# Attention decode with a cache: the last output row stored as two one-row stores from two engines, and 16 diagnostic loads taken out

## The chip, the cores and the metric

The kernel runs on one core of a Trainium2 chip. The metric is device time in microseconds (us) of one execution. A profiled execution also has a span, from its first to its last instruction, which is about 2.1 us shorter than its device time. In this kernel TensorE does the matmuls, VectorE and ScalarE make the copies, and SyncE issues most of the transfers (DMAs). SBUF is the memory that these load into, and PSUM the one that matmuls write to.

## The reference

Two decode steps for one token, side by side. A: 32 heads over 32768 cached keys. B: 32 query heads on 8 cached heads, over the last 4096 keys. Each ends with a projection from 4096 to 512 numbers, and the output is the two rows joined.

```python
def _A_ref(x, k_cache, v_cache, wq, wo):            # x [1,1,512], caches [1,32,32768,128]
    q = (x @ wq).reshape(1, 1, 32, 128).transpose(0, 2, 1, 3)
    p = softmax(einsum("bhqd,bhkd->bhqk", q, k_cache) * 128 ** -0.5)
    o = einsum("bhqk,bhkd->bhqd", p, v_cache)
    return o.transpose(0, 2, 1, 3).reshape(1, 1, 4096) @ wo        # wo [4096, 512]
# _B_ref: the same with 8 cached heads, each used by 4 query heads, and the last 4096 keys
return concatenate([a, b], axis=-1)                                # [1, 1, 1024], bf16
```

## The kernel before

It streams the caches through SBUF, one A head at a time. When the last head's cache has been asked for, SyncE asks for the output weights of B (two pieces) and A (five, growing smaller, so that little work follows the last one), and then for 16 tiny loads. Load `i` covers `i + 1` partitions with 32 bytes each. They fill a tile that nothing reads; they were put in as a diagnostic.

```python
WO_CUTS = {"A": (0, 11, 19, 25, 29, 32), "B": (0, 16, 32)}
# [...] after the loop over the A heads
for n in ("B", "A"):
    for part in range(len(self.WO_CUTS[n]) - 1):
        self.load_wo(n, part)
for i in range(16):
    self.load(self.marks[0:i + 1, 16 * i:16 * i + 16], self.X["A"]["wo"][0:i + 1, 0:16], self.marksem[i])
self.emit_spread("A")
self.emit_proj()
for i in range(16):
    self.op("sp", lambda e, i=i: e.wait_ge(self.marksem[i], 16))
for n in ("B", "A"):
    self.op("sp", lambda e, n=n: e.wait_ge(self.outsem[n], 16))
```

The projections: B first, whose four strips are summed by one more matmul; then A. Most of A's row is made as two halves of 256 columns, in partitions 0 and 64 of the PSUM bank `psPT`, by two matmuls that run side by side. One VectorE copy and one store of two rows, both 512 bytes, end the program.

```python
def halves(self, e, bank, lhsT, rhs, begin, end):
    for i in range(2):
        inst = e.matmul(bank[64 * i:64 * i + 1, 0:256], lhsT=lhsT, rhs=rhs[:, 256 * i:256 * i + 256], start=begin,
                        stop=end, tile_position=(0, 64 * i), skip_group_check=True)
    return inst

def store(self, name, bank, off, dep):
    o = self.op("dve", lambda v: v.tensor_copy(self.out_sb[0:65, :], bank[0:65, 0:256]), dep)
    self.op("sp", lambda e: e.dma_start(self.out[0, :, off:off + 512].rearrange("a (i x) -> (a i) x", i=2),
                                        self.out_sb[0:65:64, :]).then_inc(self.outsem[name], 16), o)

def emit_proj(self):
    # [...] B's 32 matmuls into self.S, in four strips
    strips = self.op("dve", lambda v: v.tensor_copy(self.pb[:, :], self.S[:, :]), o)
    rows = o = self.op("pe", lambda e: e.matmul(self.ACC[0:1, :], lhsT=self.e32[:, 0:1], rhs=self.pb[:, :], ...), strips, self.accread)
    # [...] B's copy and its store, one row of 1024 bytes, from SyncE
    row = self.proj_part("A", 0, lambda e, lhsT, rhs, a: e.matmul(self.T[1][0:1, :], ...))
    row = self.op("dve", lambda v: v.tensor_copy(self.pb[0:1, :], self.T[1][0:1, :]), row, rows)
    for part in range(1, len(self.WO_CUTS["A"]) - 1):
        if part == 3:
            self.op("pe", lambda e: self.halves(e, self.PT, self.e32[0:1, 0:1], self.pb[0:1, :], False, False), row)
        o = self.proj_part("A", part, lambda e, lhsT, rhs, a: self.halves(e, self.PT, lhsT, rhs, a == top, a == 31))
    self.store("A", self.PT, 0, o)
```

Of the kernel before, what the change touches and what calls it, by code (L numbers as in the profile page):

```python
# [3 lines left out]
BF16 = mybir.dt.bfloat16  # L4
F32 = mybir.dt.float32
ALU = mybir.AluOpType
ACTF = mybir.ActivationFunctionType
AXX = mybir.AxisListType.X

DH = 128  # L10
NQH = 32
STRIPS = 4
HALF = 128
# [40 lines left out]
class _Kernel:  # L54
# [118 lines left out]
    def emit(self, eng):  # L173
# [22 lines left out]
        def body(e):  # L196
# [30 lines left out]
            for k, plan in enumerate(plans):  # L227
                for p, q in zip(plan, plans[-1]):
                    assert p == q or (k == 0 and set(p) <= set(q)), (eng, k, p, q)
# [37 lines left out]
    def alloc(self):  # L267
        nc = self.nc
        sb = nc.alloc_sbuf_tensor
        self.kbuf = sb("kbuf", [128, 3 * HALF * DH], BF16, align_bytes=4096)  # L270
        self.vbuf = sb("vbuf", [128, 2 * HALF * DH], BF16, align_bytes=4096)
        self.kt = [sb(f"kt{i}", [128, 1024], BF16) for i in range(NKT)]
        self.psb = sb("psb", [128, 512], BF16)
        self.ptsb = sb("ptsb", [128, 512], BF16)
        self.ident = sb("ident", [128, 128], BF16)
        self.ones = sb("ones", [128, 128], BF16)
        self.e32 = sb("e32", [128, 32], F32)
        self.spread = sb("spread", [32, 4 * 129], BF16)
        self.tr = {k: sb(f"tr_{k}", [128, 32], F32) for k in ("in", "a")}
        self.rows64 = sb("rows64", [128, 64], F32)  # L280
        self.nscale = sb("nscale", [1, 128], F32)
        self.m4 = sb("m4", [1, 128], F32)
        self.pb = sb("pb", [128, 512], F32)
        self.out_sb = sb("out_sb", [128, 256], BF16)
        self.marks = sb("marks", [16, 17 * 16], BF16)
        self.c = {}
        for name, d in self.X.items():
            HG = d["HG"]
            self.c[name] = dict(
                x=sb(f"x_{name}", [128, 12], BF16),  # L290
                oc=[sb(f"oc_{name}{i}", [128, DH + 1], F32) for i in range(2 if name == "B" else 1)],
                b=sb(f"b_{name}", [128, 32], F32),
                cm=sb(f"cm_{name}", [128, 32], F32),
                mr=sb(f"mr_{name}", [1, HG], F32),
                nb=sb(f"nb_{name}", [128, 2], F32),
                hot=sb(f"hot_{name}", [128, d["nb"]], F32),
                lh=sb(f"lh_{name}", [128, HG], F32),
                hsel=sb(f"hsel_{name}", [128, 64], F32),
                rinv=sb(f"rinv_{name}", [32, 1], F32),
                ob=sb(f"ob_{name}", [32, DH], BF16),  # L300
                oz=sb(f"oz_{name}", [128, 32], BF16),
            )

        self.qz = sb("qz", [128, 32 * self.X["B"]["NKVH"] + 64], BF16)
        self.qa = sb("qa", [128, NQH], BF16)
        self.qrow = sb("qrow", [128, 512], BF16)
        self.qw = sb("qw", [128, 64], BF16)
        self.hw = sb("hw", [128, 32], F32)
        ps = nc.alloc_psum_tensor
        self.S = ps("psS", [128, 512], F32)  # L310
        self.T = [ps(f"psT{i}", [128, 512], F32) for i in range(NT)]
        self.PT = ps("psPT", [128, 512], F32)
        self.ACC = ps("psACC", [128, 512], F32)
        self.G = ps("psG", [128, 512], F32)
        s = nc.alloc_semaphore
        self.ksem = [s(f"ksem{i}") for i in range(2)]
        self.vsem = [s(f"vsem{i}") for i in range(2)]
        self.xsem = {n: s(f"xsem_{n}") for n in self.X}
        self.wosem = {n: [s(f"wosem_{n}{i}") for i in range(len(self.WO_CUTS[n]) - 1)] for n in self.X}
        self.outsem = {n: s(f"outsem_{n}") for n in self.X}  # L320
        self.marksem = [s(f"marksem{i}") for i in range(16)]



# [69 lines left out]
    def plan(self):  # L394
        self.lsem = {"k": self.ksem, "v": self.vsem}
        self.fill = {w: [0, 0] for w in "kv"}
        self.free = {"k": [None] * 3, "v": [None] * 2}
        self.nbatch = 0
        self.copies = []
        self.pending = []  # L400
        self.psread = self.ptread = self.sread = self.accread = None
        self.gath = self.qcopy = self.hcopy = self.qread = None
        self.constants()
        a, b = self.X["A"], self.X["B"]

        self.load_wq("B")
        self.load_b("k", 0)
        self.load_wq("A")
        self.load_b("k", 1)
        self.emit_qproj("B")  # L410
        self.emit_unit("B", 0)
        self.emit_qproj("A")
        self.emit_stats("B", 0)
        self.emit_unit("B", 1, {1: lambda: self.emit_PT("B", 0)})
        self.emit_stats("B", 1)
        for g in range(2):
            if g == 1:
                self.emit_PT("B", g)
            self.load_b("v", g)
            self.emit_PV("B", g)  # L420
        self.emit_spread("B")

        for g in range(NQH):
            self.loop = {"pe": g, "dve": g // 2}
            self.load_k(g, 1 if 0 < g < NQH - 1 else 2)
            self.load_v(g)
            self.emit_qcopy(g)
            self.emit_unit("A", g)
            self.emit_stats("A", g)
            self.emit_PT("A", g)  # L430
            self.emit_PV("A", g)
        self.loop = {}
        for n in ("B", "A"):
            for part in range(len(self.WO_CUTS[n]) - 1):
                self.load_wo(n, part)
        for i in range(16):
            self.load(self.marks[0:i + 1, 16 * i:16 * i + 16], self.X["A"]["wo"][0:i + 1, 0:16], self.marksem[i])
        self.emit_spread("A")
        self.emit_proj()
        for i in range(16):  # L440
            self.op("sp", lambda e, i=i: e.wait_ge(self.marksem[i], 16))
        for n in ("B", "A"):
            self.op("sp", lambda e, n=n: e.wait_ge(self.outsem[n], 16))

    def constants(self):
# [264 lines left out]
    def proj_part(self, name, part, out):  # L710

        a0, a1 = self.WO_CUTS[name][part:part + 2]
        oz, wo = self.c[name]["oz"], self.kbuf[:, HALF * DH * self.wo_third(name):]
        def mm(e):
            inst = None
            for a in range(a0, a1):
                inst = out(e, oz[:, a:a + 1], wo[:, 512 * a:512 * a + 512], a)
            return inst
        return self.op("pe", mm, (self.wosem[name][part], 16), self.c[name]["ozop"])

    def halves(self, e, bank, lhsT, rhs, begin, end):

        for i in range(2):
            inst = e.matmul(bank[64 * i:64 * i + 1, 0:256], lhsT=lhsT, rhs=rhs[:, 256 * i:256 * i + 256], start=begin,  # L724
                            stop=end, tile_position=(0, 64 * i), skip_group_check=True)
        return inst

    def store(self, name, bank, off, dep):
        o = self.op("dve", lambda v: v.tensor_copy(self.out_sb[0:65, :], bank[0:65, 0:256]), dep)  # L729
        self.op("sp", lambda e: e.dma_start(self.out[0, :, off:off + 512].rearrange("a (i x) -> (a i) x", i=2),  # L730
                                            self.out_sb[0:65:64, :]).then_inc(self.outsem[name], 16), o)

    def emit_proj(self):

        top = self.WO_CUTS["A"][1]
        for part in range(len(self.WO_CUTS["B"]) - 1):
            o = self.proj_part("B", part, lambda e, lhsT, rhs, a: e.matmul(
                self.S[32 * (a % 4):32 * (a % 4) + 1, :], lhsT=lhsT, rhs=rhs, start=(a < 4), stop=(a >= 28),
                tile_position=(0, 32 * (a % 4)), skip_group_check=True))
# [3 lines left out]
        o = self.op("dve", lambda v: v.tensor_copy(self.qrow[0:1, :], self.ACC[0:1, :]), o)  # L743
        self.op("sp", lambda e: e.dma_start(self.out[0, :, 512:1024], self.qrow[0:1, :]).then_inc(self.outsem["B"], 16), o)
        row = self.proj_part("A", 0, lambda e, lhsT, rhs, a: e.matmul(
            self.T[1][0:1, :], lhsT=lhsT, rhs=rhs, start=(a == 0), stop=(a == top - 1), skip_group_check=True))
        row = self.op("dve", lambda v: v.tensor_copy(self.pb[0:1, :], self.T[1][0:1, :]), row, rows)
        for part in range(1, len(self.WO_CUTS["A"]) - 1):
            if part == 3:
                self.op("pe", lambda e: self.halves(e, self.PT, self.e32[0:1, 0:1], self.pb[0:1, :], False, False), row)  # L750
            o = self.proj_part("A", part, lambda e, lhsT, rhs, a: self.halves(e, self.PT, lhsT, rhs, a == top, a == 31))
        self.store("A", self.PT, 0, o)

# [1 line left out]
_INS = ['A_x', 'A_k_cache', 'A_v_cache', 'A_wq', 'A_wo', 'B_x', 'B_k_cache', 'B_v_cache', 'B_wq', 'B_wo']  # L755
# [24 lines left out]
```

## Time and profile before

| | before |
|---|---|
| device time, median of 3 | 1324.14 us (1323.98 to 1324.18) |
| span of the profiled run | 1322.0 us |
| HBM read | 570.43 MB at 432 GB/s |
| last A weights land, from the span's start | 1318.87 us |
| from there to the end | 3.09 us |

Lines of the profile's page of the kernel before: the span, the mean busy share of the 16 DMA engines in 40 equal slices (in tenths), and the traffic.

```profile
span 1322.0 us, 28805 instructions
...
DMA  9999999999999999999999999999999999999998
...
HBM read 570.43 MB, written 0.00 MB: 432 GB/s over the span
```

The transfers are never below 9 tenths before the last slice. The kernel is as long as its loads, plus what follows the last one. The end of the chain of waits of the kernel before (start, duration, what) shows which load that is:

```profile
1286.51 32.36 DMA kbuf<-in_A_wo_dram
1318.87 0.04 issue
1318.92 0.51 PE psPT L724 x6
1319.43 0.02 issue
1319.45 0.42 DVE out_sb L729
```

The same end in the timeline of the kernel before (start, duration, engine, line, operation, and in brackets the idle time ahead of it with what ended it; SPq is SyncE's queue, where a DMA's issue is shown):

```profile
1287.37 20.63 SPq L326 DMA_DIRECT2D marks<-in_A_wo_dram  x15
...
1313.40 0.24 SPq L744 DMA_DIRECT2D out_dram<-qrow  x1
...
1318.92 0.20 PEld L724 LDWEIGHTS psPT<-kbuf,oz_A 128*1 128x1 bf16 x6 [0.58 <-DMA kbuf<-in_A_wo_dram]
1318.92 0.49 PE L724 MATMUL psPT<-kbuf,oz_A 128*1 128x256 bf16 x6 [0.29 <-DMA kbuf<-in_A_wo_dram]
1319.45 0.42 DVE L729 CAST out_sb<-psPT 65x256 bf16<-65x256 f32 x1 [3.71 <-PE psPT L724]
1319.90 0.59 SPq L730 DMA_DIRECT2D out_dram<-out_sb  x1
```

TensorE waits for the weights, then come copy, issue, flight and the program's end. The diagnostic loads (`marks`) are issued while SyncE has nothing else to do. The one-row store of B takes SyncE 0.24 us to issue, the two-row store of A 0.59 us.

### The profile page before, as it was taken

Reading aid. Unit: us, or ns where it says so; the run is one execution under the profiler, and the core shown is the slowest. Engines: PE = TensorE matmul, PEld = TensorE weight load, DVE = VectorE, ACT = ScalarE, POOL = GpSimd, SP = SyncE. Lnnn points to the kernel's source line nnn. Section 1 sums busy time; section 2 is a strip of 40 time slices with the busy share of each in tenths; the row PEclk is TensorE's granted clock in tenths of the full one; section 3 lists DMA queues with packets and bytes.
Section 4 is the critical chain, followed back from the end, with each engine's and each line's share of the span. In section 5 each row is a group of like instructions: output and inputs, shape, how many; then the busy total and the mean of one; then the engine's idle time right before and its main releaser. Section 6 shows DMA issues by size and latency. Waiting matters only on the chain. (4 is left out here: it accounts for less than half of the span.)

```text
span 1322.0 us, 28805 instructions
## 1 busy us (share of the span) xinstructions
PE 966.2 (73%) x13243; PEld 674.9 (51%) x13243; DVE 751.3 (57%) x1341; ACT 54.8 (4%) x167; POOL 2.6 (0%) x22
## 2 busy tenths in 40 slices
PE   4675668777767877677787876778787677868686
PEld 3453446555444655444465544446554444655453
DVE  3663456665545666554566655556655555666463
ACT  0000000000000000000000000000000000000000
POOL 0000000000000000000000000000000000000000
PEclk8887798888779887877988788798878878888798
DMA  9999999999999999999999999999999999999998
GB/s 404 434 435 435 436 432 436 434 436 434 431 436 436 428 438 434 430 438 432 434 436 432 434 434 434 436 432 434 437 430 436 436 430 436 434 432 436 432 434 359
DMA packets 13489, 570.60 MB, mean 432 GB/s; under 512 B 1827, under 2 KB 1830, under 8 KB 2214
## 3 DMA queue, kind: packets, MB, share of 16 engines
q1 hardware_dynamic: 13190, 570.44, 99.8%
q8 instruction: 8, 0.13, 0.0%
q10 hardware_dynamic: 288, 0.00, 0.0%
q14 instruction: 3, 0.02, 0.0%
HBM read 570.43 MB, written 0.00 MB: 432 GB/s over the span
## 5 line engine op out<-in xcount | busy, mean ns | idle before, releaser
L563 DVE COPY kt<-psT 128x1024 bf16<-128x1024 bf16 x1056 | 654.9, 684 | 237.5 <-PE psT L559 235.7
L559 PE MATMUL psT<-ident,kbuf 128*128 128x128 bf16 x8448 | 579.1, 234 | 168.5 <-DMA kbuf<-in_A_k_cache_dram 154.6
L559 PEld LDWEIGHTS psT<-ident,kbuf 128*128 128x128 bf16 x8448 | 539.3, 106 | 261.0 <-DMA kbuf<-in_A_k_cache_dram 162.7
L662 PE MATMUL psACC<-vbuf,ptsb 128*4 128x512 bf16 (+1 forms) x2112 | 185.2, 527 | 23.2 <-ACT ptsb L637 21.3
L582 PE MATMUL psS<-kt,qw 128*32 128x512 bf16 x2048 | 157.6, 384 | 15.3 <-DVE kt L563 15.3
L676 DVE TENSOR_SCALAR oc_A<-psACC,hot_A 128x128 f32<-128x128 f32 x32 | 11.2, 351 | 250.1 <-PE psG L689 250.1
L662 PEld LDWEIGHTS psACC<-vbuf,ptsb 128*4 128x4 bf16 (+1 forms) x2112 | 60.4, 110 | 138.2 <-issue 91.0
L610 ACT ACTIVATE psb<-psS,nb_A 128x512 bf16<-128x512 f32 x32 | 22.0, 687 | 1165.4 <-DVE nb_A L609 1165.4
L582 PEld LDWEIGHTS psS<-kt,qw 128*32 128x32 bf16 x2048 | 34.0, 95 | 57.9 <-DVE kt L563 31.3
L689 PE MATMUL psG<-oc_A,hw 128*32 128x128 f32 (+1 forms) x128 | 19.3, 227 | 52.3 <-DVE oc_A L678 52.3
L689 PEld LDWEIGHTS psG<-oc_A,hw 128*32 128x32 f32 x128 | 11.4, 109 | 62.4 <-DVE oc_A L678 55.1
L634 PE MATMUL psPT<-ident,psb 128*128 128x128 bf16 x136 | 18.0, 275 | 34.0 <-ACT psb L610 34.0
L678 DVE SCALAR_TENSOR_TENSOR oc_A<-psACC,hot_A,oc_A 128x128 f32<-128x128 f32 x96 | 33.7, 351 | 3.4
L599 DVE TENSOR_REDUCE tr_in<-psS 128x1 f32<-128x512 f32 x34 | 23.5, 692 | 17.1 <-PE psS L582 17.1
L634 PEld LDWEIGHTS psPT<-ident,psb 128*128 128x128 bf16 x136 | 10.2, 117 | 37.0 <-ACT psb L610 36.7
L603 PE MATMUL psACC<-rows,tr_in 128*1 128x64 f32 x64 | 8.7, 217 | 25.5 <-DVE tr_in L599 25.5
L637 ACT ACTIVATE ptsb<-psPT 128x512 bf16<-128x512 bf16 x34 | 20.3, 597 | 31.1 <-PE psPT L634 31.1
L603 PEld LDWEIGHTS psACC<-rows,tr_in 128*1 128x1 f32 x64 | 2.7, 80 | 35.1 <-DVE tr_in L599 35.1
L607 PE MATMUL psACC<-mr_A,nscale 1*128 1x1 f32 x64 | 12.1, 256 | 9.7 <-DVE mr_A L606 9.7
L607 PEld LDWEIGHTS psACC<-mr_A,nscale 1*128 1x128 f32 x64 | 9.4, 182 | 15.7 <-DVE mr_A L606 15.7
L609 DVE COPY nb_A<-psACC 128x1 f32<-128x1 f32 x32 | 5.0, 157 | 15.0 <-PE psACC L607 15.0
L501 PE MATMUL psACC<-vbuf,x_B 128*2 128x512 bf16 x32 | 3.6, 627 | 13.5 <-DMA x_B<-in_B_x_dram 13.5
(81 smaller groups left out, 75.7 us busy)
## 6 DMA issues: line engine op xcount, KB each, us to landing
kbuf<-in_A_k_cache_dram SPq DMA_DIRECT2D x4, 4096.0 KB, 22.2
kbuf<-in_B_k_cache_dram SPq DMA_DIRECT2D x2, 4096.0 KB, 31.7
vbuf<-in_B_v_cache_dram SPq DMA_DIRECT2D x2, 4096.0 KB, 24.7
vbuf<-in_B_wq_dram SPq DMA_DIRECT2D x1, 4096.0 KB, 12.5
vbuf<-in_A_wq_dram SPq DMA_DIRECT2D x1, 4096.0 KB, 32.2
kbuf<-in_B_wo_dram SPq DMA_DIRECT2D x2, 2048.0 KB, 33.3
kbuf<-in_A_wo_dram SPq DMA_DIRECT2D x1, 1408.0 KB, 27.7
kbuf<-in_A_wo_dram SPq DMA_DIRECT2D x1, 1024.0 KB, 29.7
```

The lines of the kernel that those rows point to most:

```text
L559: inst = e.transpose(T[:, 128 * k:128 * k + 128], src[:, DH * k:DH * k + DH], self.ident[:, :])
L563: self.copies.append(self.op("dve", lambda v: v.tensor_copy(KT[:, :], T[:, :]), o, to="pe"))
L582: inst = e.matmul(self.S[32 * c:32 * c + 32, :], lhsT=win, rhs=self.kt[(bb + c // 2) % NKT][:, 512 * (c % 2):512 * (c % 2) + 512], start=b ...
L599: o = dve(lambda v: v.reduce_max(tr["in"][:, 0:1], self.S[:, :], axis=AXX), self.sdone, self.k_pool, to="pe" if name == "A" else None)
L603: o = self.op("pe", lambda e: e.matmul(self.ACC[0:1, 0:64], lhsT=tr["in"][:, 0:1], rhs=self.rows64[:, :], start=True, stop=True, skip_grou ...
L607: o = self.op("pe", lambda e: e.matmul(self.ACC[:, 64:65], lhsT=self.nscale[:, :], rhs=t["mr"][0:1, :], start=True, stop=True, skip_group_ ...
L610: self.sread = self.op("act", lambda s: s.activation(out=self.psb[:, :], in_=self.S[:, :], func=ACTF.Exp, bias=t["nb"][:, k:k + 1], scale= ...
L634: inst = e.transpose(PT[:, 128 * jj:128 * jj + 128], self.psb[:, 128 * jj:128 * jj + 128], self.ident[:, :])
L637: self.ptread = self.op("act", lambda s: s.activation(out=self.ptsb[:, :], in_=PT[:, 0:512], func=ACTF.Copy), self.psread, to="pe")
L662: inst = e.matmul(acc[32 * c:32 * c + rows, 0:512], lhsT=lhsT, rhs=rhs, start=begin, stop=end, tile_position=(0, 32 * c), skip_group_check ...
L678: o = self.op("dve", lambda v, src=src, hot=hot: v.scalar_tensor_tensor(out=oc, in0=src, scalar=hot, in1=oc, op0=ALU.mult, op1=ALU.add), p ...
L689: return self.op("pe", lambda e: e.matmul(self.G[0:32, c0 + c:c0 + c2], lhsT=win, rhs=t["oc"][g % len(t["oc"])][:, c:c2], start=False, sto ...
```

## The change

Its intent: drop the diagnostics, and shorten the end. Each half of the row gets its own matmul signal, its own copy (VectorE and ScalarE side by side) and its own one-row store (from SyncE and ScalarE).

```diff
 [...]
-        for i in range(16):
-            self.load(self.marks[0:i + 1, 16 * i:16 * i + 16], self.X["A"]["wo"][0:i + 1, 0:16], self.marksem[i])
         self.emit_spread("A")
         self.emit_proj()
-        for i in range(16):
-            self.op("sp", lambda e, i=i: e.wait_ge(self.marksem[i], 16))
-        for n in ("B", "A"):
+        for n in self.outsem:                    # "B", "A0", "A1"
             self.op("sp", lambda e, n=n: e.wait_ge(self.outsem[n], 16))
 [...]
-    def store(self, name, bank, off, dep):
-        o = self.op("dve", lambda v: v.tensor_copy(self.out_sb[0:65, :], bank[0:65, 0:256]), dep)
-        self.op("sp", lambda e: e.dma_start(self.out[0, :, off:off + 512].rearrange("a (i x) -> (a i) x", i=2),
-                                            self.out_sb[0:65:64, :]).then_inc(self.outsem[name], 16), o)
+    def store(self, bank, i, dep):
+        row = slice(64 * i, 64 * i + 1)
+        out, src = self.out_sb[row, :], bank[row, 0:256]
+        if i == 0:
+            o = self.op("dve", lambda v: v.tensor_copy(out, src), dep)
+        else:
+            o = self.op("act", lambda e: e.activation(out=out, in_=src, func=ACTF.Copy), dep)
+        self.op("act" if i else "sp", lambda e: e.dma_start(self.out[0, :, 256 * i:256 * i + 256], out).then_inc(
+            self.outsem[f"A{i}"], 16), o)
 [...]
-            o = self.proj_part("A", part, lambda e, lhsT, rhs, a: self.halves(e, self.PT, lhsT, rhs, a == top, a == 31))
-        self.store("A", self.PT, 0, o)
+            self.proj_part("A", part, lambda e, lhsT, rhs, a: self.halves(e, self.PT, lhsT, rhs, a == top, False)
+                           if a < 31 else None)
+        oz, wo = self.c["A"]["oz"], self.kbuf[:, HALF * DH * self.wo_third("A"):]
+        for i in range(2):
+            o = self.op("pe", lambda e, i=i: self.halves(e, self.PT, oz[:, 31:32], wo[:, 512 * 31:512 * 32], False, True, (i,)),
+                        (self.wosem["A"][-1], 16), self.c["A"]["ozop"])
+            self.store(self.PT, i, o)
```

More of the change, by code (lines that the diff above doesn't have):

```diff
@@ L284, in alloc @@
         self.out_sb = sb("out_sb", [128, 256], BF16)
-        self.marks = sb("marks", [16, 17 * 16], BF16)
         self.c = {}
@@ L319, in alloc @@
         self.wosem = {n: [s(f"wosem_{n}{i}") for i in range(len(self.WO_CUTS[n]) - 1)] for n in self.X}
-        self.outsem = {n: s(f"outsem_{n}") for n in self.X}
-        self.marksem = [s(f"marksem{i}") for i in range(16)]
+        self.outsem = {n: s(f"outsem_{n}") for n in ("B", "A0", "A1")}
     def load(self, dst, src, sem, *deps):
@@ L716, in mm, with halves @@
             for a in range(a0, a1):
-                inst = out(e, oz[:, a:a + 1], wo[:, 512 * a:512 * a + 512], a)
+                inst = out(e, oz[:, a:a + 1], wo[:, 512 * a:512 * a + 512], a) or inst
             return inst
-        return self.op("pe", mm, (self.wosem[name][part], 16), self.c[name]["ozop"])
-    def halves(self, e, bank, lhsT, rhs, begin, end):
-        for i in range(2):
+        deps = (self.wosem[name][part], 16), self.c[name]["ozop"]
+        return self.op("pe", mm, *deps)
+    def halves(self, e, bank, lhsT, rhs, begin, end, only=(0, 1)):
+        for i in only:
             inst = e.matmul(bank[64 * i:64 * i + 1, 0:256], lhsT=lhsT, rhs=rhs[:, 256 * i:256 * i + 256], start=begin,
```

## The prediction

> **What bounds the kernel now.** Its loads. The page shows 570.43 MB read from HBM at 432 GB/s over 1322.0 us, and the DMA row of the 40 slices stands at 9 tenths in all but the last. The chain of waits agrees for the end: 32.36 us of it is the last piece of the A output weights, landing at 1318.87. Only what follows can shrink: TensorE 0.51 us, VectorE's copy 0.42 (from 1319.45), the store's issue on SyncE 0.59 (from 1319.90), its flight, and the program's end at 1321.96. That is 3.1 us, 0.23%.
>
> **Removed: 16 diagnostic loads.** The timeline shows SyncE issuing them from 1286.99 to 1308.0, behind all the A weights; SyncE has nothing else to do then. Their 136 packets of 32 bytes follow the weights on each DMA engine, so the weights should not land sooner. Their completions run until 1320.64 and hold back the B store (issued 1313.40, complete 1320.53), which isn't last. The A store's packets start at 1321.13, 0.64 us after its issue ends; the very first load, on empty queues, needed 0.61 (0.43 to 1.04). So the loads don't hold up the A store either. The waits for them occupy SyncE from 1320.53 to 1320.99, but the A store completes only at 1321.49: hidden. Removal alone: 0.0 us (up to 0.1).
>
> **Changed at the end.** The two last matmuls ran side by side (starts 1319.135 and 1319.138), so a signal for each half gains nothing. VectorE's copy of 1x256 should cost what 65x256 does (1x512 took 0.68 us, 128x512 0.69): 0.42 us. ScalarE: 0.195 us for one column and 0.687 for 512 give an estimate of 0.44 for 256, so it is ready with VectorE or 0.03 later.
>
> The gain is in the issue: 0.59 us for the two-row store, 0.24 for the one-row B store. A one-row store should start its packet 0.35 us sooner. The Trainium skill ("DMA: Bandwidth & Descriptors", "Why a DMA increments its semaphore by 16 and not by 1") has such a store use one engine, the sequencer adding the other counts; the trace agrees: the B store is one packet of 1024 bytes with one completion. The same page ("Issuing engines are not separate DMA queues") says that issuing from two engines saves only sequencer time. Simultaneous issues from both at the start took 0.34 to 0.59 us, so I allow 0.1 us for the pair's interference. Both packets go to one engine, 0.03 us each. The completion that ends the program is probably ScalarE's.
>
> **Sum.** 0.35 less 0.03 to 0.1: 0.25 to 0.3 us, 0.02%. From 1324.14 I predict 1323.86 us; 8 in 10 between 1323.3 and 1324.3. Faster by over 2%: 0.003; within 2%: 0.994; slower: 0.003.
>
> **What would show it.** Right: the last weights land at 1318.9 again; copies on VectorE and ScalarE overlap, 0.42 to 0.44 us; each store's issue takes 0.25 to 0.4; last completion about 1321.2, span 1321.7; the B store completes near 1315. Wrong: weights over 0.2 us sooner (the loads did cost something), or an issue on ScalarE of 0.6 us.
>
> **What would make it wrong.** A reload of ScalarE's table before its copy (1.28 us at the start; in the loop it copies without one); the two issues taken one after the other; a different pace of the loads over 1320 us, where 0.05% exceeds the whole change.

## The result, and the profile after

The changed kernel took 1323.68 us (median of 6, 1323.58 to 1326.17) and the kernel before 1324.16 us (median of 6, 1323.98 to 1324.72). The ratio is 1.0, 95% interval 0.9987 to 1.0013: the same, by that measure. It isn't the ratio of the medians, which is 0.9996: the means of the six runs are equal (1324.22 us each), since one run at 1326.17 us pulls that of the changed kernel up.

Lines of the page after:

```profile
span 1321.6 us, 28783 instructions
...
DMA  9999999999999999999999999999999999999998
...
HBM read 570.43 MB, written 0.00 MB: 432 GB/s over the span
```

The load pace is untouched. The end in the timeline after:

```profile
1314.71 0.32 SPq L744 DMA_DIRECT2D out_dram<-qrow  x1
...
1318.89 0.20 PEld L719 LDWEIGHTS psPT<-kbuf,oz_A 128*1 128x1 bf16 x6 [0.26 <-DMA kbuf<-in_A_wo_dram]
1319.42 0.41 DVE L727 CAST out_sb<-psPT 1x256 bf16<-1x256 f32 x1 [2.36 <-PE psPT L719]
1319.45 0.38 ACT L729 ACTIVATE out_sb<-psPT 1x256 bf16<-1x256 f32 x1 [18.04 <-PE psPT L719]
1319.86 0.25 SPq L730 DMA_DIRECT2D out_dram<-out_sb  x1
1319.86 0.58 ACTq L730 DMA_DIRECT2D out_dram<-out_sb  x1
```

The weights are still what TensorE waits for last (0.26 us), but in this execution its weight loads (PEld) sat idle for only 0.26 us there, against 0.58 before. The end of the chain of waits after therefore runs back through TensorE's earlier work and not through the load:

```profile
1316.24 3.15 PE psPT L719 x42
1319.39 0.02 issue
1319.42 0.41 DVE out_sb L727
```

That chain hides a wait which the timeline shows. It is a warning that will matter below: in this execution the loads lead TensorE by very little.

The trace also records when a store's packets (the pieces in which it is moved) start and when its completion (the last count on the semaphore that the program waits for) arrives. All times are us from the span's start:

| step | before | after, half from SyncE | after, half from ScalarE |
|---|---|---|---|
| last A weights land | 1318.874 | 1318.848 | 1318.848 |
| last matmul starts | 1319.138 | 1319.109 | 1319.112 |
| copy starts, takes | 1319.452, 0.421 | 1319.417, 0.411 | 1319.451, 0.375 |
| issue starts, takes | 1319.900, 0.592 | 1319.856, 0.249 | 1319.856, 0.583 |
| first packet starts | 1321.125 | 1320.572 | 1320.683 |
| completion | 1321.493 | 1320.927 | 1321.111 |
| end of the trace | 1321.961 | 1321.585 | 1321.585 |

I call U the time from the start of the last matmul to the end of the trace. It leaves out whatever made that matmul early or late. U fell from 2.823 to 2.473 us, by 0.350 us, and the columns before and ScalarE's give its parts as differences. The copy and what leads to the issue: 0.018 less. Issue to packet: 1.225 to 0.827, 0.398 less. Packet to completion: 0.368 to 0.428, 0.060 more. The end: 0.006 more. So the gain lies between the start of the issue and the first packet.

### The profile page after: what moved, and what is told of

Same layout as the page of the kernel before. It is cut to its first block, busy times and chain, and to the rows that moved or that the text cites. A ratio compares the mean times of both kernels' runs of the same rounds, so it can differ in the third digit from the quotient of the medians.

```text
span 1321.6 us, 28783 instructions
## 1 busy us (share of the span) xinstructions
PE 969.7 (73%) x13243; PEld 676.6 (51%) x13243; DVE 751.8 (57%) x1341; ACT 55.2 (4%) x168; POOL 2.6 (0%) x22
```

## The experiments

My theory was that a one-row store starts its packet sooner than a two-row one and that all else is worth nothing. Rivals: the diagnostic loads were the cost; the copies side by side are the gain. Twelve kernels ran, in three groups, each group on one chip with the kernel before beside it. All gave correct results. The device times differ by less than their scatter, so each profile's U decides, and the times are given beside it. That is one profile per kernel, but U repeats well: it was 2.473 to 2.481 us in the seven profiles of the changed and the reordered end (after, e0, e7 to e11), and 2.816 to 2.847 in the three with a two-row store (before, e1, e3).

| run | U, us | last matmul after last landing, us | median, us | fastest, us |
|---|---|---|---|---|
| before, first profile | 2.82 | 0.26 | 1324.16 | 1323.98 |
| changed, first profile | 2.47 | 0.26 | 1323.68 | 1323.58 |
| group 1: before | | | 1324.31 | 1323.84 |
| e0_after | 2.48 | 1.38 | 1323.86 | 1323.54 |
| e1_no_loads | 2.82 | 0.26 | 1324.02 | 1323.83 |
| e2_loads_kept | 2.46 | 0.79 | 1323.89 | 1323.57 |
| e3_two_row | 2.85 | 0.26 | 1324.09 | 1323.98 |
| group 2: before | | | 1324.09 | 1323.90 |
| e4_both_sync | 2.60 | 0.26 | 1324.05 | 1324.01 |
| e5_both_act | 2.86 | 0.59 | 1324.29 | 1324.10 |
| e6_one_copy | 2.61 | 0.26 | 1324.38 | 1323.82 |
| e7_reorder | 2.48 | 0.26 | 1323.85 | 1323.72 |
| group 3: before | | | 1324.29 | 1323.74 |
| e8_after_again | 2.48 | 0.26 | 1323.82 | 1323.55 |
| e9_reorder_again | 2.48 | 0.26 | 1323.65 | 1323.43 |
| e10_late | 2.48 | 2.58 | 1325.96 | 1324.77 |
| e11_late_reorder | 2.48 | 1.86 | 1325.10 | 1324.17 |

Every ratio to the kernel before had an interval that holds 1 (from 0.9995 for e0_after and e2_loads_kept to 1.0011 for e10_late).

### e0_after: the changed kernel again

No edit. 

> The changed kernel again, unedited, on the same chip as the next three. T is the time from the landing of the last piece of the A output weights to the end of the trace; it was 3.09 us before the change (1318.874 to 1321.961) and 2.74 after it (1318.848 to 1321.585). Both theories: T 2.74 within 0.05; device time 0.3 to 0.5 us under the kernel before.

The time behaved (0.45 us under before, by medians), but the profile fell in an execution of 1324.68 us, and T, the measure I had announced, was 3.86 us and not 2.74. Lines of the timeline of e0_after:

```profile
1319.45 0.63 PEld L719 LDWEIGHTS psPT<-kbuf,oz_A 128*1 128x1 bf16 x14 [0.44 <-issue]
1319.45 0.93 PE L719 MATMUL psPT<-kbuf,oz_A 128*1 128x256 bf16 x14
1320.41 0.41 DVE L727 CAST out_sb<-psPT 1x256 bf16<-1x256 f32 x1 [2.23 <-PE psPT L719]
```

The last 14 matmuls run in one go, with no wait for weights ahead of them; these had landed at 1318.73. TensorE's own chain was late. From its last matmul on, all went as before: U 2.48. My expectation of T was wrong, because I had taken the landing of the weights for the only thing that sets the last matmul's start. From here on I use U, and call an execution lucky when the weights, and not TensorE's chain, come last.

### e1_no_loads: only the diagnostic loads are removed

```diff
 # the kernel before [...]
-        for i in range(16):
-            self.load(self.marks[0:i + 1, 16 * i:16 * i + 16], ..., self.marksem[i])
 [...]
-        for i in range(16):
-            self.op("sp", lambda e, i=i: e.wait_ge(self.marksem[i], 16))
```

> The kernel before without its 16 diagnostic loads and their waits, the last store as it was (one VectorE copy, one two-row store from SyncE). My theory (the gain is in the store's issue; the loads were hidden): T stays 3.09 within 0.06, the time equals the kernel before within 0.15 us, and only the B store's completion moves, from 3.1 us after its packet to about 0.5. Rival (the loads and their waits were the cost): T about 2.75, time 0.35 us or more under before, and the last weights may land sooner.

U 2.816 and T 3.08: the loads and their waits cost nothing, and the rival falls. The median, 0.29 us under that of before, was outside my 0.15; the fastest runs, 1323.83 and 1323.84, agree. Five of the nine runs of before took 1324.31 us or more; no profile was kept of those, so that they were late as e0 was is likely and not shown. B's store completed 0.48 us after its packet, where it had taken 3.22 (packet at 1317.305, completion at 1320.528); with the loads back (e2) it took 3.21. So the loads did hold something up: the completion of B's store, which wasn't last. The weights landed at 1318.655, 0.22 us sooner than before, which is the prediction's own sign that the loads had cost something. But in e2, with all the loads, they landed at 1318.671, so the loads don't explain it. Over all 14 profiles the landing lay between 1318.60 and 1319.07, a scatter of 0.47 us that is larger than the gain.

### e2_loads_kept: only the store is changed

```diff
 # the changed kernel [...]
+        for i in range(16):
+            self.load(self.marks[0:i + 1, 16 * i:16 * i + 16], ..., self.marksem[i])
         self.emit_spread("A")
         self.emit_proj()
+        for i in range(16):
+            self.op("sp", lambda e, i=i: e.wait_ge(self.marksem[i], 16))
```

> The changed kernel with the 16 diagnostic loads and their waits put back. My theory: T about 2.75 to 2.9, time 0.2 to 0.4 us under before. The range allows for this: [...]completions of these loads ran until 1.77 us after the last weights' landing, and the new packets start 1.72 us after it, so the loads that were hidden behind the slow store may show a little behind the fast one. Rival (the loads were the cost): T about 3.09, as before.

U 2.461, the whole gain with all the loads in place. T was 3.25, above the range and indeed above before's, since TensorE's chain was late. The end of the timeline of e2_loads_kept has the issues of the changed kernel:

```profile
1320.20 0.24 SPq L736 DMA_DIRECT2D out_dram<-out_sb  x1
1320.20 0.58 ACTq L736 DMA_DIRECT2D out_dram<-out_sb  x1
```

Why the chain was late can be read here, and it isn't as in e0. B's projection started at 1309.31 us, sooner than in the lucky profile after (1310.26), but its 32 matmuls took 3.31 us in place of 1.90: the granted clock was 0.5 from 1308.80 to 1312.22, and 1.0 there in the profiles of before, after and e0. From the start of B's projection to the last matmul e2 needed 10.15 us, and the two other late profiles, e0 and e5, 8.73. The profile was of a late execution, so the loads had 0.5 us more time to finish; whether they show in a lucky one can be read only from the fastest times, 1323.57 against 1323.54 for the changed kernel: no sign of it.

### e3_two_row: split copies, one two-row store

```diff
 # the changed kernel, store(): both copies as they were, then
-        self.op("act" if i else "sp", lambda e: e.dma_start(self.out[0, :, 256 * i:256 * i + 256], out)...)
+        self.op("sp", lambda e: e.dma_start(self.out[0, :, 0:512].rearrange("a (i x) -> (a i) x", i=2),
+                                            self.out_sb[0:65:64, :]).then_inc(self.outsem["A"], 16), self.half, o)
```

> The changed kernel with its two copies on VectorE and ScalarE, but one two-row store from SyncE that waits for both. My theory: the split copy gains nothing and the two-row issue takes 0.59 us again, so T 3.05 to 3.12 and the time is that of before within 0.15 us. Rival (the copies side by side are the gain): T about 2.75, time 0.35 us under before.

U 2.847, T 3.11. The timeline of e3_two_row:

```profile
1319.34 0.41 DVE L727 CAST out_sb<-psPT 1x256 bf16<-1x256 f32 x1 [2.26 <-PE psPT L719]
1319.38 0.38 ACT L729 ACTIVATE out_sb<-psPT 1x256 bf16<-1x256 f32 x1 [17.97 <-PE psPT L719]
1319.83 0.59 SPq L730 DMA_DIRECT2D out_dram<-out_sb  x1
```

The copies overlap as in the changed kernel, and the two-row issue takes 0.59 us again, its packet 1.227 us after the issue's start. All of the gain is gone. The side-by-side copies by themselves gain nothing.

### e4_both_sync: two one-row stores, both from SyncE

```diff
-        self.op("act" if i else "sp", lambda e: e.dma_start(
+        self.op("sp", lambda e: e.dma_start(
```

> The changed kernel, both one-row stores from SyncE, one after the other. U is the time from the start of the last matmul to the end of the trace: 2.82 us before the change, 2.47 after it, 2.46 with the loads kept, 2.85 with one two-row store. My theory (a one-row issue costs SyncE 0.25 us, and what ends the program is the later store's completion): the second issue starts 0.3 us after the first, so its packet starts about 0.15 to 0.2 us later than ScalarE's did (0.83 us after the first issue's start): U 2.6 to 2.7. Rival (only the number of rows in a store matters, not who issues): U 2.47. Second rival (two rows cost the same however they are issued): U 2.82.

U 2.596, at the near end of the range. Both issues in the timeline of e4_both_sync:

```profile
1320.08 0.54 SPq L730 DMA_DIRECT2D out_dram<-out_sb  x2
```

The second issue started 0.293 us after the first, and each packet came 0.72 us after its own issue. So one-row stores alone are worth 0.23 us of the 0.35, and issuing the second from another engine 0.12. The device times, 1324.05 against 1324.09 for before, don't show the 0.23; in this profile the weights landed at 1319.07, 0.2 us later than before and the latest of all profiles, for which I have no cause.

### e5_both_act: both from ScalarE

```diff
 # the changed kernel, store(): both copies as they were, then
+        for j, d in enumerate((self.half, o)):
+            self.op("act", lambda e, j=j: e.dma_start(self.out[0, :, 256 * j:256 * j + 256],
+                    self.out_sb[64 * j:64 * j + 1, :]).then_inc(self.outsem[f"A{j}"], 16), d)
```

> Both one-row stores from ScalarE, after its copy. It tells why ScalarE's issue took 0.58 us where SyncE's took 0.25. If ScalarE is slow at issuing by itself, two issues take 1.2 us, and U is 2.9 to 3.2. If its 0.58 us was the wait for SyncE's simultaneous issue, each takes 0.25 to 0.3, and U is 2.6 to 2.7, as with both from SyncE.

U 2.856: neither alternative as I put it. Both issues in the timeline of e5_both_act:

```profile
1320.08 0.81 ACTq L731 DMA_DIRECT2D out_dram<-out_sb  x2
```

The first issue took 0.509 us with SyncE silent, the second 0.257. Yet the first packet came 0.751 us after its issue's start, nearly as soon as SyncE's. So ScalarE's first issue is long by itself (the simultaneous one adds 0.07 us), and the length matters for what ScalarE issues next and little for that packet. Why the first is long is left open.

### e6_one_copy: one copy, two one-row stores from SyncE

```diff
-            o = self.op("dve", lambda v: v.tensor_copy(out, src), dep)      # and ScalarE's copy
+        o = self.op("dve", lambda v: v.tensor_copy(self.out_sb[0:65, :], bank[0:65, 0:256]), dep)
+        for j in range(2):
+            self.op("sp", lambda e, j=j: e.dma_start(self.out[0, :, 256 * j:256 * j + 256],
+                    self.out_sb[64 * j:64 * j + 1, :]).then_inc(self.outsem[f"A{j}"], 16), o)
```

> One VectorE copy of 65x256 as before the change, and two one-row stores from SyncE. My theory (the split copy gains nothing): U equal to that of the run with both stores from SyncE and split copies, within 0.04 us. Rival (the split copy gains): U 0.1 us or more longer than that.

U 2.611, 0.015 us from e4's. The split copy is worth nothing; it only has ScalarE's row ready on ScalarE.

### e7_reorder and e9_reorder_again: filling TensorE's idle time

```diff
         strips = self.op("dve", lambda v: v.tensor_copy(self.pb[:, :], self.S[:, :]), o)
+        row = self.proj_part("A", 0, lambda e, lhsT, rhs, a: e.matmul(self.T[1][0:1, :], ...))
         rows = o = self.op("pe", lambda e: e.matmul(self.ACC[0:1, :], ...), strips, self.accread)
 [...]
-        row = self.proj_part("A", 0, lambda e, lhsT, rhs, a: e.matmul(self.T[1][0:1, :], ...))
```

> The changed kernel with one more edit: the 11 matmuls of the first piece of the A projection are issued ahead of the row sum of B, so TensorE has work in the 1.3 us in which it waited for VectorE's copy of B's strips. It tests my reading of the late runs: in three of the six profiles the last matmul started 0.04 us after the last weights' landing plus 0.2 us of earlier matmuls; in the unlucky ones (the changed kernel's repeat was 1.0 us later, the one with the loads kept 0.4) TensorE's chain from the last head was late, with the weights landed as always. If so, this gives a late run back up to about 1 us: U stays 2.47, the last matmul starts 0.25 us after the last landing, median 1323.4 to 1323.7, and fewer runs over 1324. If late runs come from the loads, the spread of its times is as that of the changed kernel, and the last matmul is late by as much as before.

> The reordered kernel once more (its first five runs lay within 0.16 us, but its profile fell in a lucky execution, so they showed little). If the order shortens a late chain by about 1 us: all five within 0.3 us, the same fastest run as the changed kernel within 0.1 us, and a lower or equal median. If its narrow spread was luck: a run 0.5 us or more over the fastest, as with the changed kernel.

(Four, not three, of the six profiles before this run started the last matmul 0.26 us after the landing.) The first five runs lay between 1323.72 and 1323.88, the next five between 1323.43 and 1323.93. The first median missed my 1323.4 to 1323.7. The second set missed too: its spread of 0.50 us is over the 0.3 that I had set and just reaches the 0.5 that I had named as the sign of luck, and its fastest run lies 0.12 us from e8's, not within 0.1; only the median was lower, as expected. Side by side in group 3, the reordered kernel's mean is 1323.68 us and that of the changed one (e8) 1323.97. Over all its sets, the changed kernel had 6 of 16 runs over 1324.0 us; the reordered one had none of 10. These sets mix chips and groups (in group 3 alone it is 2 of 5 against none of 5), so that the order removes late runs is likely and not shown. Both its profiles fell in lucky executions and prove nothing of the cause; the next pair tests what the order is worth when the chain is late.

### e8_after_again: the changed kernel on the chip of group 3

No edit. 

> The changed kernel once more, for the same chip as the next. Two profiles of it so far had the last matmul 0.26 and 1.38 us after the last landing of weights. Expected: fastest run 0.3 to 0.4 us under the fastest of before, U 2.47, and at least one of five runs 0.5 us or more over its fastest, if TensorE's chain is late in some runs as I read it.

Fastest 1323.55 us, 0.19 under the fastest of before (a little less than expected), and two of five runs 0.85 us or more over it, as expected.

### e10_late and e11_late_reorder: a late chain, on purpose

```diff
 # the changed kernel (e10), the reordered kernel (e11)
-        for part in range(len(self.WO_CUTS["B"]) - 1):
+        for part in (0, 0, 0, 1):
```

> The changed kernel with the first half of the B projection done three times instead of once (the result is the same, since each pass starts its sums anew): TensorE's chain is made late by about 1.9 us (two more passes of 16 matmuls; 32 took 1.9 us). If the end is the later of the weights' landing and TensorE's chain, with 1.2 us of slack in a lucky run: time 0.5 to 2.0 us over the changed kernel's, with the weights landing as always and U 2.47. If only the weights' landing counts: the same time.

> The same lateness put into the reordered kernel. If the order fills 1.0 us of TensorE's idle time: 0.8 to 1.1 us under the run with the lateness alone in a case where that one is 1 us or more late, and its last matmul that much nearer to the last landing. If the order gains nothing: the same time as that run.

Weights landed as always (1318.73 and 1318.83), U was 2.48 in both, and the times rose to 1325.96 and 1325.10 us: the first 2.1 us over e8, just past the top of my range, the second 0.86 less. B's projection in the timeline of e10_late, with what TensorE does next:

```profile
1310.85 3.62 PE L737 MATMUL psS<-kbuf,oz_B 128*1 128x512 bf16 x64
...
1315.28 1.02 PE L741 MATMUL psACC<-pb,e 128*1 128x512 f32 x2 [0.80 <-DVE pb L740]
...
1316.13 2.11 PE L745 MATMUL psT<-kbuf,oz_A 128*1 128x512 bf16 x9
```

The same place in the timeline of e11_late_reorder:

```profile
1311.21 3.62 PE L737 MATMUL psS<-kbuf,oz_B 128*1 128x512 bf16 x64
...
1314.66 2.54 PE L741 MATMUL psT<-kbuf,oz_A 128*1 128x512 bf16 x11
```

From the start of B's projection to the last matmul, e10 needed 10.46 us and e11 9.48. The wait for VectorE's copy (0.80 us of idle TensorE) is filled. This shows that the end of the kernel is the later of two things, the weights' landing and TensorE's chain. What makes the chain late without such an edit is settled for e2 alone, where a stretch of half clock lay on B's projection. In e0 and e5 B's projection itself started late (1311.38 and 1310.60). Its start moves with the stretches in which the trace shows a granted clock of 0.5: in the first two profiles and e0, the last such stretch before B's projection ended at 1304.55, 1305.95 and 1307.15 us, and B's projection started at 1308.94, 1310.26 and 1311.38. Which of them drives the other, no run here tells.

## Why the prediction was right or wrong

- **Bound by the loads; 3.1 us at stake.** Right for the load pace and for the profiled executions. Incomplete: TensorE's chain is a close second and comes last in some executions (seen in the profiles of e0, e2 and e5; 6 of the changed kernel's 16 runs took over 1324.0 us, of which only e0's has a profile). The prediction saw the scatter only as "a different pace of the loads"; the profiles of e0 and e2 show unchanged landings and late matmuls. The landings do scatter as well, by 0.47 us, so that warning was half of the matter.
- **Removing the loads gains 0.0 us.** Right: U 2.82 without them (e1) and 2.46 with them beside the new store (e2). That they held back the B store was right too. That it would complete near 1315 was wrong: it completed at 1317.49, since its packet only started at 1317.01. I had read the delay as the loads' alone.
- **Copies and matmuls side by side gain nothing.** Right: e3 (2.85 against 2.82) and e6 against e4 (2.61 against 2.60). The last two matmuls again started 0.003 us apart. ScalarE's copy took 0.375 us, less than the estimate of 0.44.
- **The gain is in the issue, 0.35 us, less 0.03 to 0.1 for the pair.** The place was right and the sum close (U fell by 0.350, against 0.25 to 0.3), but its terms were mis-sized and cancelled, so the closeness of the sum is partly luck. I took the packet to start about 0.6 us after an issue's end, so that the shorter issue was the gain. SyncE's issue was indeed 0.34 us shorter, but its packet also started sooner after the issue's end. The two-row packet came 1.225 us after its issue's start and SyncE's one-row packet 0.716: 0.51 sooner, not 0.35. Why the second row costs that much isn't shown: the two-row store also has two packets and two completion counts where a one-row store has one, and no run tells these apart. Against that stood 0.11 for ScalarE's later packet and 0.06 for its slower completion, where I had allowed 0.1 at most.
- **An issue of 0.6 us on ScalarE would show it wrong.** ScalarE's took 0.583 and the gain came all the same; the sign was badly chosen. The length of an issue isn't the time to its packet: ScalarE's packet started 0.24 us after the end of its issue, SyncE's 0.47, the two-row store's 0.63. The Trainium skill ("DMA: Bandwidth & Descriptors", "Issuing engines are not separate DMA queues") says that issuing from several engines saves only sequencer time. e4 agrees and puts a number to it: 0.12 us.
- **1323.86 us, 8 in 10 between 1323.3 and 1324.3.** Measured 1323.68. The range also holds the time of the kernel before (1324.16), so to land in it proves little; the test of the prediction is U. The difference of the medians, 0.48 us, is more than U's 0.35; the rest is within the scatter, since the fastest runs differ by 0.40, 0.30 and 0.19 us in the three sets of rounds that hold both kernels.

## What to carry to other kernels

A last store costs from the start of its issue to its completion; compare shapes by the time to the packet and from there to the completion, and not by how long the issuing engine is busy: here two rows from one issue took 1.23 us to the first packet, one row from SyncE 0.72. Diagnostics that come after the last useful load can be free even where they hold up other completions; ask which wait ends last. And when a gain is below the scatter, measure from the last event that both versions share, and find out what the scatter is: here it was in part a second chain of work just behind the first. Reordering 11 matmuls gave 0.86 us back when that chain was made late on purpose; that it takes the late runs away otherwise isn't shown.

## What the Trainium skill lacked or had wrong

- "DMA: Bandwidth & Descriptors", "Latency and other measured facts" and "Specifications" give about 600 ns to the first byte for DMAs issued from SyncE and ScalarE, whatever the shape. Neither says from which moment they count. Here the first packet came 0.72 us after the start of a one-row issue from SyncE, 0.75 from ScalarE alone, and 1.22 to 1.23 us for two rows (three profiles); from the issue's end it was 0.47, 0.24 and 0.63. That a second row costs 0.5 us isn't on the page.
- The same page, "Issuing engines are not separate DMA queues", has no durations of an issue, and the page's only figures for one from SyncE or ScalarE are sequencer cycles in its part on trn3. Here: one row from SyncE 0.24 to 0.32 us, two rows 0.59, one row from ScalarE 0.51 the first time (0.58 beside SyncE's) and 0.26 directly after it.
- The same page, "Anatomy of one DMA", puts most of about 2 us into the write receipt, for DMAs from GpSimd. For the 512-byte stores here, from SyncE and ScalarE, packet start to completion was 0.35 to 0.44 us. The page has no figure for how far other DMAs stretch it: with 16 loads of 32 bytes per partition around it, a 1024-byte store needed 3.2 us in place of 0.48.
